# Scaled K and scaled R turned by one transposing DMA in place of two, and w_in loaded in three parts

## The chip, the cores and the metric

The kernel runs on one core of a Trainium2 chip. The core has five engines that run on their own and wait for each other through semaphores: PE (TensorE, matrix multiply), DVE (VectorE), ACT (ScalarE), POOL (GpSimd) and SP (SyncE, which only issues DMAs here). Sixteen DMA engines move data; SP's DMAs, POOL's DMAs and the fetches of the program itself all go through them. The metric is device time in microseconds, median of the runs shown; less is better.

## The reference

Two stages follow each other. The first is a linear attention with a decaying state, for 4 sequences of 768 steps, 8 heads of 48:

```
state = 0
for t in range(768):
    cur    = u * k[t] (outer) v[t]
    y[t]   = r[t] @ (state + cur)
    state  = w * state + k[t] (outer) v[t]
```

The second is a two-layer network on the 3072 rows of y (384 columns): `h = x @ w_in` (384 to 2048), a gate that is 0 below -1, h above 1 and (h+1)^2/4 between, and `g @ w_out` (2048 to 384). Inputs and output are float32.

## The kernel before

**Tiling.** The attention is done in chunks of 128 steps. There are 6 chunks and two pairs of sequences, so 12 groups g = 0 to 11; group g is chunk g // 2 of sequence pair g % 2. A group has two units (one sequence each), n = 2g and 2g + 1. Tokens of a unit stand on the 128 partitions when loaded: K, R and V of a group are 128 x 16 heads x 48 float32, three DMAs from SP (`load.K`, `load.R`, `loadV`; from group 2 on, one DMA for both units).

**Attention of a unit.** K and R are multiplied by tables of powers of w (L327), which gives Ks and Rs in bfloat16, padded from 48 to 64 columns a head so that two heads fill 128. Ks and Rs are turned (tokens from partitions to columns): for groups 0 to 2 on PE (L388, then a copy TT), from group 3 on by a transposing DMA from SP, one for Ks and one for Rs (step KRT, L398), each 128 x 1024 bfloat16. Then A = turned K times turned R (L406), its masked copy AT, Y = AT times V plus turned R times the state (L441, L446), and the state's update (Sp L432, Tm, decay). The bonus of u goes over KU, RKU, diag and V2 on POOL, DVE and ACT. y (L468) is Y + V2; from group 3 on both units' y stand in one tile yy and are turned by a further transposing DMA (xT, L511).

**Network of a group.** Per group: four quarters q of 512 hidden columns. mm1 (L526, 12 matmuls of 256 columns a quarter), relu and square on ACT, gate on DVE, then mm2 (L554) for each unit and quarter; `o` copies the result and `out` stores it. w_in lies whole in SBUF, loaded by POOL DMAs in W_IN = 2 parts of 1024 columns; w_out in 4 parts.

**Order.** The order of all work is written out by hand in the table ORDER: each token is one step, the digits behind its colon are buffer numbers, and each engine takes its own instructions in the order of the tokens. An engine, SP among them, stops at the first instruction whose wait is not fulfilled; what stands behind it on that engine stays back. Writing `KRT.K.4` means the turning DMA of Ks of group 4.

In the text a DMA is named by its step and group: KT.4 and RT.4 are the two turning DMAs of group 4, VF.3 is the load of V of group 3, xT.4 the turning of yy of group 4, w_out.2 the third part of w_out.

Of the kernel before, what the change touches and what calls it, by code (L numbers as in the profile page):

```python
# [36 lines left out]
lw loadV.0.0:0 bcw:1 load.K.1.1 KU.0.1@D loadV.0.1 wcol:0 Wdn_p:0 Ks.0.0@D:0 Wup_p load.R.1.1 Rs.0.0@D:0 wCm  # L37
KU.1.0@P:1 loadV.1.0:1 Ks.1.0@D:1 warm.4.h.2 T.0:1 load.K.2.0:2 Wdn RKU.1.0@P:1 Rs.1.0@D:1 Rs.0.1@D V.0.0@A:0
RKU.0.1@P T.2:2~3 TT.0@A:0 usum.0.0@D:0 Ks.1.1@D Ks.0.1@D KU.1.1@P Wup Sp.0:0 TT.2@D:1 A.0:1 V.0.1@A load.R.2.0:2
AT.0.1:0 RKU.1.1@P Tm.0@D Sp.1:1~5 T.1:2 Tm.1@D w_in.0 V.1.0@A:1 A.2:1 Rs.1.1@D loadV.1.1 Sp.2:0 AT.0.0 TT.1@D:2  # L40
usum.1.0@A:1 A.1:0~8 V2.0.0@P:0 Ks.2.0@P:2 AT.2.0:1 loadV.2.0:0 V2.1.0@A:1 Y.0:1 T.3:2 sbf.0@A Tm.2@D usum.0.1@D Y.2:0
TT.3@D:3 y.2:0 AT.1.1:2 Rs.2.0@P:2 A.3:1~14 X.2:0 V2.0.1@A y.0:1 AT.3.0:3 warm.2.h.2 X.0:1 T.5:2~8 AT.1.0 xT.2@A:0
T.4:0 TT.5@D:0 Y.1:0 w_in.1 load.K.3.0:0 xT.0@A:1 sbf.1@A usum.1.1@D A.5:1 mm1.0.0.0:2 KU.2.0@P:0 y.1:2 TT.4@D:1
load.R.3.0:0 V.1.1@A X.1:1 Y.3:0 AT.5.0:0 A.4:0 V2.1.1@P xT.1@A mm1.0.0.1 V.2.0@A:2 Sp.5:1 y.3:0 RKU.2.0@P:0
relu.0.0:0 X.3:0 Tm.5@D:0 mm1.0.1.0:1 AT.4.0:1 xT.3@A decay.5 square.0.0:0 usum.2.0@D:0 Sp.4:1 mm1.0.1.1 w_out.0 Y.4:0
relu.0.1:1 mm1.1.1.-1:0 gate.0.0:0 square.0.1:1 Tm.4@D:1 mm1.0.2.-1:2 relu.1.1:0 Y.5:1 square.1.1:0 V2.2.0@P:0 w_out.1
y.4:1 gate.0.1:1 w_out.2 X.4:0 w_out.3 mm1.0.3.-1:1 xT.4@A:2 gate.1.1:2 relu.0.2:1 Sp.3:0 y.5:2 mm1.1.0.-1:0
square.0.2:1 Tm.3@D KU.3.0@P:1 decay.4 gate.0.2:3 relu.0.3:0 relu.1.0:1 mm2.0.0.0:1 mm2.0.1.0:0 Ks.3.0@P:0
square.1.0:0 KRT.K.3:0 mm1.1.3.-1:2 mm2.0.1.1 Rs.3.0@P:0 RKU.3.0@P:1 mm2.0.0.1 square.0.3:1 gate.1.0:4 mm2.0.1.2 gate.0.3:5
relu.1.3:1 loadV.3.0:1 mm2.0.0.2 mm1.1.2.-1:0 square.1.3:0 usum.3.0@D:1 mm2.0.0.3 relu.1.2:0 KRT.R.3:0 mm2.0.1.3  # L50
o.0.0@D:0 square.1.2:1 mm2.1.0.0:1 o.0.1@D gate.1.3:6 load.K.4.0:1 X.5:0 mm2.1.0.1 load.R.4.0:1 xT.5@A V.3.0@A:3
mm1.2.3.-1:1 gate.1.2:7 sbf.3@A V2.3.0@P:1 Sp.7:0 A.7:2 loadV.4.0:0 relu.2.3:1 Tm.7@D:0 A.6:0 mm2.1.0.2 AT.6.0:2
sbf.2@A square.2.3:0 Ks.4.0@P:2 sbf.4@A Sp.6:0 mm2.1.0.3 load.K.5.0:2 Tm.6@D:1 mm1.2.0.-1:0 o.1.0@A:1 AT.7.0:3 decay.6
Y.6:0 Y.7:1 relu.2.0:0 KRT.K.4:1 y.6:0 mm1.2.1.-1:2 KU.4.0@P:0 y.7 V.4.0@A:4 gate.2.3:8 xT.6:1 RKU.4.0@P:0
square.2.0:1 mm2.1.1.0:0 Sp.8:1 mm2.1.1.1 load.R.5.0:2 Tm.8@D:1 relu.2.1:1 load.K.6.0:0 mm1.2.2.-1:1 gate.2.0:9
Ks.5.0@P:1 mm2.1.1.2 square.2.1:0 mm2.2.0.0:1 mm2.1.1.3 decay.7 Rs.4.0@P:1 mm1.3.0.-1:0 gate.2.1:0 relu.2.2:0
square.2.2:1 KRT.K.5:0 mm2.2.0.1 o.1.1@D sbf.5@A relu.3.0:1 mm1.3.1.-1:2 gate.2.2:1 out.1 KU.5.0@P:1 square.3.0:0
Rs.5.0@P:2 mm2.2.0.2 relu.3.1:0 gate.3.0:3 mm1.3.2.-1:1 KRT.R.4:1 square.3.1:1 loadV.5.0:1 load.R.6.0:0 usum.4.0@D:0
mm2.2.0.3 mm2.2.1.0:0 KU.6.0@P:0 relu.3.2:1 gate.3.1:5 mm1.3.3.-1:0 square.3.2:0 loadV.6.0:0 gate.3.2:4 mm2.2.1.1
V2.4.0@P:0 sbf.6@A o.2.0@A:1 A.9:2 sbf.7@A relu.3.3:0 A.8:1 AT.9.0:1 mm2.2.1.2 KRT.R.5:0 square.3.3:1 mm2.3.0.0:1  # L60
AT.8.0:0 out.0 decay.8 mm2.2.1.3 load.K.7.0:1 mm2.3.0.1 o.2.1@A gate.3.3:2 V.6.0@A:0 V.5.0@A:2 Y.8:0 Ks.6.0@P:0
mm2.3.0.2 y.8:1 Y.9:0 mm2.3.0.3 y.9 RKU.5.0@P:1 A.11:2 xT.8:0 o.3.0@A:0 A.10:1 usum.5.0@D:1 AT.11.0:2 mm2.3.1.0:0
Sp.10:1 KRT.K.6:1 mm2.3.1.1 Rs.6.0@P:0 RKU.6.0@P:0 Tm.10@D:0 mm2.3.1.2 load.R.7.0:1 Sp.9:1 mm2.3.1.3 Tm.9@D:1
V2.5.0@P:1 mm1.4.0.-1:0 AT.10.0:3 o.3.1@A sbf.8@A decay.9 decay.10 KRT.R.6:1 usum.6.0@D:0 relu.4.0:1 Sp.11:1 Y.10:0
mm1.4.1.-1:2 square.4.0:0 Tm.11@D:1 y.10:0 V2.6.0@P:0 Ks.7.0@P:2 Y.11:1 mm1.4.2.-1:1 loadV.7.0:0 out.2 relu.4.1:0
# [5 lines left out]
relu.5.1:1 xT.12:1 gate.5.2:8 mm2.4.1.0:1 KU.8.0@P:0 Sp.14:0 square.5.1:0 mm2.4.1.1 load.K.9.0:0 Tm.14@D:1 mm2.4.1.2
relu.5.3:0 sbf.10@A gate.5.1:3 mm2.5.0.0:0 Rs.8.0@P:2 A.15:2 square.5.3:1 A.14:0 AT.15.0:3 mm2.4.1.3 mm2.5.0.1
V.8.0@A:3 KRT.R.8:1 decay.13 RKU.8.0@P:0 AT.14.0:2 mm1.6.0.-1:2 o.4.1@A load.R.9.0:0 gate.5.3:5 Y.14:1 mm2.5.0.2
Ks.9.0@P:0 y.14:0 relu.6.0:1 mm1.6.1.-1:0 square.6.0:0 usum.8.0@D:0 gate.6.0:4 loadV.9.0:0 load.K.10.0:1 mm2.5.0.3
mm2.5.1.0:1 sbf.11@A sbf.12@A A.17:1 relu.6.1:0 o.5.0@D:0 KU.9.0@P:1 A.16:2 mm2.5.1.1 AT.17.0:0 V2.8.0@P:0 decay.14
Rs.9.0@P:0 square.6.1:1 sbf.13@A Y.15:0 mm2.5.1.2 mm1.6.2.-1:1 y.15 V.9.0@A:4 AT.16.0:1 xT.14:0 KRT.K.9:0 Sp.15:0
RKU.9.0@P:1 gate.6.1:2 mm2.5.1.3 load.R.10.0:1 mm1.6.3.-1:2 relu.6.2:1 square.6.2:0 relu.6.3:0 o.5.1@D Tm.15@D:0
mm2.6.0.0:1 gate.6.2:7 out.5 Y.16:0 mm1.7.1.-1:0 decay.15 square.6.3:1 y.16:1 KRT.R.9:0 Ks.10.0@P:2 Sp.17:0 Tm.17@D:1
gate.6.3:6 load.K.11.0:2 mm2.6.0.1 relu.7.1:1 mm1.7.0.-1:1 KU.10.0@P:0 square.7.1:0 sbf.15@A mm2.6.0.2 Sp.16:0
relu.7.0:0 KRT.K.10:1 loadV.10.0:1 gate.7.1:9 mm1.7.2.-1:2 Rs.10.0@P:1 Tm.16@D:0 mm2.6.0.3 square.7.0:1 o.6.0@A:0  # L80
sbf.14@A usum.9.0@D:1 Y.17:0 mm1.7.3.-1:0 decay.16 y.17 relu.7.2:1 gate.7.0:0 RKU.10.0@P:0 mm2.6.1.0:1 square.7.2:0
Sp.18:0 KRT.R.10:1 mm2.6.1.1 Tm.18@D:0 sbf.16@A decay.17 A.18:1 gate.7.2:1 out.4 mm2.7.0.0:0 relu.7.3:0 xT.16:2
KU.11.0@P:1 mm2.6.1.2 square.7.3:1 AT.18.0:2 V2.9.0@P:1 mm2.7.0.1 load.R.11.0:2 loadV.11.0:0 Ks.11.0@P:1 mm2.6.1.3
gate.7.3:3 mm2.7.0.2 A.21:2 sbf.17@A V.10.0@A:2 o.6.1@A A.19:1 AT.21.0:3 A.20:0 mm2.7.0.3 AT.19.0:1 out.6 Y.18:1
# [19 lines left out]
def kernel(  # L104
# [70 lines left out]
    for i in range(3):  # L175
        for x in padded:
            nc.vector.memset(padded[x][i][:, :, D:], 0.0)
# [472 lines left out]
```

## Time and profile before

| | us |
|---|---|
| median of 3 runs | 175.38 |
| lowest, highest | 174.95, 176.0 |
| span of the profiled execution | 176.4 |
| PE busy in it | 165.0 (94%) |
| DVE / ACT / POOL busy | 130.3 / 135.2 / 120.2 |
| clock granted to PE, mean over the span | 0.987 |
| SP's DMA queue (q1), POOL's (q0), share of 16 engines' span | 73.6% / 11.4% |

The profiled execution is given by its span alone; it is 1.0 us above the median and 0.4 us above the highest of the runs. Busy time of PE is modelled, so small waits can hide in it. DMA shares go by the time that packets were under way, two of which can overlap on an engine, so shares above 100% occur. A "group" line of the profile gives a line of the kernel, the engine, what is written and read, the count, busy time and the idle time just before.

### The profile page before, as it was taken

To read this page: it belongs to the slowest core of one execution; us is meant where nothing else is said; L and a number is where in the kernel's file an instruction comes from. 1 tells how busy PE (TensorE), PEld (TensorE's weight loads), DVE (VectorE), ACT (ScalarE), POOL (GpSimd) and SP (SyncE) were. 2 spreads that over 40 slices of the span, in tenths; PEclk is the share of its full clock that TensorE was granted. 3 is DMA by queue.
4 is the path that set the end of the run, shared out by engine and by line. 5 is a ranking of instruction groups with operands and counts; after the bars stand their busy time and mean duration, and the time that the engine had idled before them with its cause. 6 is when DMAs were issued, how large, how long until landed. Compare 5 with 4: busy or idle time off the path is not lost.

```text
span 176.4 us, 4159 instructions
## 1 busy us (share of the span) xinstructions
PE 165.0 (94%) x1684; PEld 125.2 (71%) x1684; DVE 130.3 (74%) x167; ACT 135.2 (77%) x194; POOL 120.2 (68%) x97
## 2 busy tenths in 40 slices
PE   6998699999999999779999999999999999999992
...
PEclk9999999999999999969999999999999999999998
DMA  5999999999999999996999997989982400312022
GB/s 109 221 219 192 216 175 234 207 165 209 238 172 196 191 202 252 158 183 175 196 221 211 185 183 159 266 149 243 194 197 93 89 17 4 97 37 89 4 89 89
DMA packets 106967, 28.78 MB, mean 163 GB/s; under 512 B 100930, under 2 KB 106180, under 8 KB 106948
## 3 DMA queue, kind: packets, MB, share of 16 engines
q1 hardware_dynamic: 103888, 25.24, 73.6%
q0 software_dynamic: 2912, 3.15, 11.4%
q8 instruction: 13, 0.21, 0.5%
...
q14 instruction: 6, 0.05, 0.1%
...
## 4 chain that ended last, share of the span: by engine, by line
PE 71%; DMA 13%; DVE 7%; ACT 5%; POOL 1%; issue 1%; DVEq 0%; POOLq 0%
PE hp L526 31%; PE op L554 30%; DMA VF<-in_v_dram 5%; DMA w_out_sb<-in_moe_w_out_dram 4%; DMA xT<-yy 3%; DVE AT L421 3%; PE A L406 2%; PE Y L446 2%; PE Y L441 2%; PE Sp L432 1%; ACT V L212 1%; PE ub L242 1%; POOL V L369 1%; PE wb L237 1%; ACT RKU L355 1%; DVE yy L468 1%
## 5 line engine op out<-in xcount | busy, mean ns | idle before, releaser
L526 PE MATMUL hp<-xT,w_in_sb 128*128 128x256 bf16 (+1 forms) x600 | 72.0, 271 | 3.4 <-DMA xT<-yy 2.2
L554 PE MATMUL op<-w_out_sb,gt 128*128 128x384 bf16 (+2 forms) x400 | 71.9, 320 | 0.1
L544 DVE SCALAR_TENSOR_TENSOR gt<-sq,hp 128x1024 bf16<-128x1024 f32 x48 | 57.9, 1216 | 16.2 <-ACT sq L539 16.1
L526 PEld LDWEIGHTS <-w_in_sb 128*128 128x128 bf16 x600 | 56.2, 99 | 13.9 <-issue 3.1
L534 ACT ACTIVATE pt<-hp 128x1024 f32<-128x1024 f32 x48 | 48.7, 1018 | 17.7 <-PE hp L526 17.4
L539 ACT ACTIVATE sq<-pt 128x1024 f32<-128x1024 f32 x48 | 50.4, 1057 | 1.2
L554 PEld LDWEIGHTS <-gt 128*128 128x128 bf16 x400 | 36.5, 98 | 19.3 <-issue 0.5
L421 DVE TENSOR_TENSOR AT<-A,umask 128x1024 bf16<-128x1024 f32 x22 | 26.5, 1218 | 2.2 <-PE A L406 1.9
L337 POOL TENSOR_TENSOR KU<-K,u_bc 128x768 f32<-128x768 f32 (+1 forms) x13 | 21.6, 1658 | 2.0 <-DVE u_bc L212 2.0
L344 POOL TENSOR_TENSOR RKU<-R,KU 128x768 f32<-128x768 f32 (+1 forms) x14 | 22.2, 1589 | 0.3
L489 POOL TENSOR_TENSOR state<-Tm,wCm 128x384 f32<-128x384 f32 x16 | 16.0, 1003 | 8.8 <-DVE Tm L476 8.6
L369 POOL TENSOR_TENSOR V<-V,diag 128x768 f32<-128x768 bf16 (+1 forms) x12 | 16.4, 1365 | 7.1 <-ACT V L212 4.7
L327 POOL TENSOR_TENSOR Ks<-Wdn,K 128x768 bf16<-128x768 f32 x10 | 18.2, 1818 | 1.2 <-DMA K<-in_k_dram 1.2
L327 POOL TENSOR_TENSOR Rs<-Wup,R 128x768 bf16<-128x768 f32 x10 | 18.2, 1819 | 0.1
L476 DVE TENSOR_TENSOR Tm<-Sp,state 128x384 f32<-128x384 f32 x16 | 8.9, 555 | 7.3 <-POOL Ks L327 3.4
L468 DVE TENSOR_TENSOR yy<-Y,V 128x384 bf16<-128x384 f32 x18 | 9.9, 554 | 5.0 <-PE Y L446 3.5
L212 ACT CAST V<-VF 128x768 bf16<-128x768 f32 (+1 forms) x14 | 10.2, 737 | 3.6 <-DMA VF<-in_v_dram 3.5
L446 PE MATMUL Y<-V,AT 128*128 128x48 bf16 x192 | 11.4, 185 | 1.2 <-POOL AT L416 0.9
L446 PEld LDWEIGHTS <-AT 128*128 128x128 bf16 x192 | 9.8, 98 | 2.8 <-POOL AT L416 1.3
L357 DVE TENSOR_REDUCE diag<-RKU 128x16 f32<-128x768 f32 (+1 forms) x13 | 11.1, 852 | 0.9 <-POOL RKU L344 0.9
L212 ACT COPY oo<-op 128x384 f32<-128x384 f32 x13 | 6.2, 476 | 6.7 <-PE op L554 6.3
L212 ACT CAST state_bf<-state 128x384 bf16<-128x384 f32 x20 | 10.0, 503 | 0.0
...
## 6 DMA issues: line engine op xcount, KB each, us to landing
...
```

The lines of the kernel that those rows point to most:

```text
L212: nc.scalar.copy(out, in_) if e == "A" else engines[e].tensor_copy(out, in_)
L327: engines[e].tensor_mul(of_unit(dst, j0, j1)[:, :, :, :D], rep(tab, j1 - j0), of_unit(tiles[what, g], j0, j1))
L337: engines[e].tensor_mul(of_unit(tiles["KU", g], j0, j1), of_unit(tiles["K", g], j0, j1), rep(u_bc, j1 - j0))
L344: engines[e].tensor_mul(of_unit(tiles["RKU", g], j0, j1), of_unit(tiles["R", g], j0, j1), of_unit(tiles["KU", g], j0, j1))
L369: engines[e].tensor_mul(tiles["V2", g][:, hs, :], tiles["V", g][:, hs, :], tiles["diag", g][:, hs].unsqueeze(2).to_broadcast([P, hs.stop - ...
L421: nc.vector.tensor_mul(t.rearrange("p i n t -> p (i n) t"), tiles.pop(("A", n)).rearrange("p i n t -> p (i n) t"), umask.unsqueeze(1).to_b ...
L446: nc.tensor.matmul(t[:, 2 * p + i, :], tiles["AT", n][:, i, p, :], tiles["V", g][:, j * H + 2 * p + i, :], start=(c == 0), stop=True, skip ...
L526: nc.tensor.matmul(hp[:, f, cols], w_in_sb[:, i, n0 : n0 + P], tiles["xT", g][:, units, i, :], start=(i == 0), stop=(i == nK - 1), skip_gr ...
L534: nc.scalar.activation(tiles["pt", g, q], tiles["hp", g, q], AF.Relu, bias=0.5, scale=0.5)
L539: nc.scalar.activation(tiles["sq", g, q], tiles.pop(("pt", g, q)), AF.Square, bias=0.0)
L544: nc.vector.scalar_tensor_tensor(out=gt, in0=tiles.pop(("sq", g, q)), scalar=1.0, in1=tiles.pop(("hp", g, q)), op0=ALU.min, op1=ALU.max)
L554: nc.tensor.matmul(t, tiles["gt", g, q][:, f, j * P : (j + 1) * P], w_out_sb[:, n, cols], start=(n == 0), stop=(n == nF - 1),)
```

## The change

There are four edits. (1) The padded buffers of Ks and Rs become one tile KRs (128 x 2 x 16 x 64) with Ks in its first half and Rs in its second; the six memsets of the padding on DVE become three of twice the width. (2) The step KRT turns the whole tile with one DMA (128 x 2048) into KRT, from which A and Y read K's and R's part. (3) In ORDER the token `KRT.K.g` is gone and `KRT.g` stands where `KRT.R.g` stood, which is behind the scaling of R. (4) W_IN lists column bounds: parts of 512, 512 and 1024 columns; `w_in.1` stands right behind `w_in.0`, and `w_in.2` where the second part stood.

```diff
-W_IN = 2
+W_IN = (0, 512, 1024, 2048)
 ...
-AT.0.1:0 RKU.1.1@P Tm.0@D Sp.1:1~5 T.1:2 Tm.1@D w_in.0 V.1.0@A:1 ...
+Tm.0@D Sp.1:1~5 T.1:2 Tm.1@D w_in.0 w_in.1 V.1.0@A:1 ...
 ...
-    padded = {x: [const.tile([P, UNITS * H, HP], BF16, name=x, tag=f"{x}{i}") for i in range(3)] for x in ("Ks", "Rs")}
+    padded = [const.tile([P, 2, UNITS * H, HP], BF16, name="KRs", tag=f"KRs{i}") for i in range(3)]
     for i in range(3):
-        for x in padded:
-            nc.vector.memset(padded[x][i][:, :, D:], 0.0)
+        nc.vector.memset(padded[i].rearrange("p k h d -> p (k h) d")[:, :, D:], 0.0)
 ...
     def w_in_go(e, bk, i):
-        n = slice(i * DF // W_IN, (i + 1) * DF // W_IN)
+        n = slice(W_IN[i], W_IN[i + 1])
 ...
     def scaled(e, bk, g, j, what):
         j0, j1 = span(g, j)
-        if j == 0:
-            tiles[what + "s", g] = padded[what + "s"][bk[0]]
+        if ("Ks", g) not in tiles:
+            tiles["KRs", g] = padded[bk[0]]
+            tiles["Ks", g], tiles["Rs", g] = padded[bk[0]][:, 0], padded[bk[0]][:, 1]
 ...
-        return tiles[what + "T", g][:, j * NP + p, :]
+        return tiles["KRT", g][:, "KR".index(what) * UNITS * NP + j * NP + p, :]
 ...
     @step
-    def KRT(e, bk, what, g):
-        t = tiles[what + "T", g] = buf(bk[0], [P, UNITS * NP, P], BF16, what + "T")
-        nc.sync.dma_start_transpose(out=t, in_=flat(tiles[what + "s", g]))
+    def KRT(e, bk, g):
+        t = tiles["KRT", g] = buf(bk[0], [P, 2 * UNITS * NP, P], BF16, "KRT")
+        nc.sync.dma_start_transpose(out=t, in_=tiles["KRs", g].rearrange("p k h d -> p (k h d)"))
```

The order of instructions moves on SP at nine places. The first is group 3. On SP before (names with buffer numbers; R_501 is the load of R of group 3, VF_779 that of V, KT_741 and RT_808 the two turnings, K_826 the load of K of group 4):

```order
L304 DMA K_467<-in_k_dram 128x16x48
L304 DMA R_501<-in_r_dram 128x16x48
L398 DMA_TRANSPOSE KT_741<-Ks_99 128x8x128
L304 DMA VF_779<-in_v_dram 128x16x48
L398 DMA_TRANSPOSE RT_808<-Rs_102 128x8x128
L304 DMA K_826<-in_k_dram 128x16x48
```

and the same place now (R_496 and VF_772 are the loads of R and V of group 3, KRT_801 the turning of both, K_819 the load of K of group 4):

```order
L301 DMA K_462<-in_k_dram 128x16x48
L301 DMA R_496<-in_r_dram 128x16x48
L301 DMA VF_772<-in_v_dram 128x16x48
L396 DMA_TRANSPOSE KRT_801<-KRs_99 128x16x128
L301 DMA K_819<-in_k_dram 128x16x48
```

The load of V of group 3 stood behind KT.3, which waits for POOL's scaling of K; now it stands right behind the load of R, and the turning follows it.

The second place is the turning of groups 4 and 5 and the turning of yy of group 4 on SP. Before (KT_1062 and RT_1194 are group 5, RT_1114 is group 4, xT_1273 is xT.4, K_1211 and R_1315 loads of group 7, KT_1300 is group 6):

```order
L398 DMA_TRANSPOSE KT_1062<-Ks_100 128x8x128
L587 DMA out_0_dram<-oo_925 128x2x384
L398 DMA_TRANSPOSE RT_1114<-Rs_103 128x8x128
L304 DMA VF_1118<-in_v_dram 128x16x48
L304 DMA R_1120<-in_r_dram 128x16x48
L304 DMA VF_1154<-in_v_dram 128x16x48
L398 DMA_TRANSPOSE RT_1194<-Rs_104 128x8x128
L587 DMA out_0_dram<-oo_814 128x2x384
L304 DMA K_1211<-in_k_dram 128x16x48
L511 DMA_TRANSPOSE xT_1273<-yy_1242 128x6x128
L398 DMA_TRANSPOSE KT_1300<-Ks_99 128x8x128
L304 DMA R_1315<-in_r_dram 128x16x48
```

and now (KRT_1103, KRT_1183 and KRT_1336 are groups 4, 5 and 6, xT_1262 is xT.4, K_1200 and R_1302 the loads of group 7):

```order
L585 DMA out_0_dram<-oo_918 128x2x384
L396 DMA_TRANSPOSE KRT_1103<-KRs_100 128x16x128
L301 DMA VF_1107<-in_v_dram 128x16x48
L301 DMA R_1109<-in_r_dram 128x16x48
L301 DMA VF_1143<-in_v_dram 128x16x48
L396 DMA_TRANSPOSE KRT_1183<-KRs_101 128x16x128
L585 DMA out_0_dram<-oo_807 128x2x384
L301 DMA K_1200<-in_k_dram 128x16x48
L509 DMA_TRANSPOSE xT_1262<-yy_1231 128x6x128
L301 DMA R_1302<-in_r_dram 128x16x48
L396 DMA_TRANSPOSE KRT_1336<-KRs_99 128x16x128
```

The K halves have moved back to the places of the R halves, and behind xT.4 stands a load where a turning stood.

The third place is POOL at the first part of w_in. Before:

```order
L344 TENSOR_TENSOR RKU_209<-R_156,KU_187 128x384
L290 DMA w_in_sb_66<-in_moe_w_in_dram 128x3x1024
L416 AFFINE_SELECT AT_255<-AT_255 128x1024
L369 TENSOR_TENSOR V2_327<-V_213,diag_230 128x384
L327 TENSOR_TENSOR Ks_101<-Wdn_127,K_206 128x16x48
```

and now:

```order
L342 TENSOR_TENSOR RKU_203<-R_150,KU_181 128x384
L287 DMA w_in_sb_66<-in_moe_w_in_dram 128x3x512 x2
L414 AFFINE_SELECT AT_249<-AT_249 128x1024
L367 TENSOR_TENSOR V2_322<-V_207,diag_224 128x384
L325 TENSOR_TENSOR KRs_101<-Wdn_121,K_200 128x16x48
```

Two DMAs of half the columns stand on POOL where one stood; the rest of POOL's order is as it was.

More of the change, by code (lines that the diff above doesn't have):

```diff
@@ L36 @@
 warm.18 load.K.0.0:0 load.R.0.0:0 load.K.0.1 load.R.0.1 load.K.1.0:1 load.R.1.0:1 bcu:0 u_bc@D KU.0.0@P:0 RKU.0.0@P:0
[L37 to L65, printed above, removed]
@@ L71 @@
[L71 to L84, printed above, removed]
-o.7.0@A:1 y.18:0 mm1.8.0.-1:2 relu.8.0:1 KRT.K.11:0 AT.20.0:0 Y.19:0 mm1.8.1.-1:1 y.19 mm2.7.1.0:1 square.8.0:0
```

78 lines of the change are left out of this document (60 added, 18 removed).

## The prediction

> **What bounds the kernel now.** I read the page's first two parts, then the chain of waits, then the stretches in which PE is not busy.
>
> ```profile
> span 176.4 us, 4159 instructions
> PE 165.0 (94%) x1684; PEld 125.2 (71%) x1684; DVE 130.3 (74%) x167; ACT 135.2 (77%) x194; POOL 120.2 (68%) x97
> ...
> PE   6998699999999999779999999999999999999992
> ...
> PEclk9999999999999999969999999999999999999998
> DMA  5999999999999999996999997989982400312022
> ```
>
> A slice is 4.4 us. PE is full from slice 5 (22 us) on, with one hole at slices 16 and 17 (70 to 79 us), where its clock drops too. The DMA engines are full from the start to about 110 us. So there are three stages: a start up to 40 us that hangs on DMA, a middle up to 80 us in which PE is full but for one hole, and the rest, which is PE alone. A change to DMAs can matter in the start and at the hole. The chain, cut to 14 to 42 us, shows what the start hangs on:
>
> ```profile
> 28.04 1.47 POOL V L369
> 29.50 0.76 POOL w_out_sb L294
> 30.26 7.92 DMA w_out_sb<-in_moe_w_out_dram
> 38.22 1.46 PE op L554 x8
> ```
>
> The start ends when w_out.2 has landed at 38.18 and PE's second layer reads it. The 7.92 us are mostly queueing: the DMA queues in 27 to 30 us and in 30.5 to 37.5 us (packets, MB, share) were
>
> ```profile
> q1 hardware_dynamic: 3500, 0.67, 113.0%
> q0 software_dynamic: 42, 0.05, 10.0%
> ```
>
> ```profile
> q0 software_dynamic: 1836, 1.37, 127.9%
> ```
>
> First SP's queue (q1: K and R of group 3) has the engines to itself, although w_out.0 was issued at 26.91 (below); then POOL's (q0: w_out) has them, 262 packets a us, so 1.95 us for each of its four parts of 512 packets.
>
> The hole, by the chain, PE's timeline, and stretches (length, busy time of PE, PEld, DVE, ACT, POOL, then clock, DMA share, GB/s):
>
> ```profile
> 69.89 6.13 DMA xT<-yy
> ```
>
> ```profile
> 73.07 0.81 PE L554 MATMUL op<-w_out_sb,gt 128*128 128x384 bf16 x4
> 76.06 2.72 PE L526 MATMUL hp<-xT,w_in_sb 128*128 128x256 bf16 x12 [2.18 <-DMA xT<-yy]
> ```
>
> ```profile
> 74.00:75.00 1.00, 0.00 (x0) 0.00 (x0) 1.00 (x2) 0.81 (x2) 1.00 (x2) 1.00 0.00 0
> ```
>
> ```profile
> 75.00:80.00 5.00, 3.94 (x33) 3.15 (x33) 1.61 (x3) 1.15 (x2) 4.96 (x4) 0.66 0.91 177
> ```
>
> PE waits 2.18 us for xT.4, and then gets 0.66 of its clock over 5 us, which loses 0.34 x 5 = 1.7 us more: 3.9 us in all. xT.4 took 6.13 us where its kind takes 2.7 to 2.8 (below), and in 74 to 75 us no DMA packet started at all. What stopped them? The DMA view of 73.2 to 73.3 us and of 60.5 to 61.5 us, the other place where packets of a turning DMA stopped:
>
> ```profile
> q8 instruction: 1, 0.02, 108.6%
> ```
>
> ```profile
> q8 instruction: 1, 0.02, 5.9%
> ```
>
> ```profile
> q8 instruction: 13, 0.21, 0.5%
> ```
>
> Both times one packet of the instruction queue (the last row is the page's: 13 packets, 16 KB each, about one for each 259 of PE's 1684 matmuls and as many weight loads) went out while a turning DMA was under way, and the turning stood still until it was through. I read it so: a turning goes in step over all engines, so one engine held by a fetch holds all. The fetch comes when PE reaches a certain instruction; xT.4 comes when yy is done. Whether they meet is a matter of some tenths of a us, and this decides 3.9 us.
>
> **The change part by part.** The turning DMAs, by tile:
>
> ```profile
> L398 SPq DMA_TRANSPOSE KT<-Ks x9: 1242/1324/3627, 36.3 to 127.6; - x9
> ...
> DMA to landing us min/median/max: 2.8/4.5/5.4
> ```
>
> ```profile
> DMA to landing us min/median/max: 2.7/4.7/5.5
> ```
>
> ```profile
> DMA to landing us min/median/max: 2.7/2.8/6.1
> ```
>
> The fences are KT, RT and xT. An issue of 256 KB keeps SP for 1.24 us at least. I take twice that for the whole tile (2.5 us; the same rows would have to be described), so nine turnings fewer save SP nothing, and the DMA engines move the same packets. Bounds: nothing is saved, or 9 x 1.24 = 11 us of SP, which waits much of its time anyway. On the path either counts zero, except at the following places.
>
> *Start: V of group 3 goes ahead of w_out.* SP's timeline:
>
> ```profile
> 22.46 4.37 SPq L304 DMA_DIRECT2D R<-in_r_dram  x1
> 36.34 1.32 SPq L398 DMA_TRANSPOSE KT<-Ks  x1
> 37.78 0.51 SPq L304 DMA_DIRECT2D VF<-in_v_dram  x1
> ```
>
> SP stood from 26.83 to 36.34 in front of KT.3, which waits for POOL, with VF.3 behind it. Without KT.3, VF.3 is issued at 26.83, eleven us earlier. It is 2048 packets, which at 3500 in 3 us are 1.75 us of all engines, and now they fall between the loads of group 3 and w_out, whose landing PE waits for. If SP's queue goes first, as it did in 27 to 30 us, w_out moves by 1.75 us; if the two take turns, packet for packet, by what passes while w_out.0 to .2 go, three quarters of it, 1.3 us. Lower end 0 (the engines would have to have room; the share of 127.9% speaks against it), upper end 1.75. I take 1.6, nearer the first, since that is what the 42 packets of q0 show. What is gained: V of group 3 is cast earlier, which lets POOL's V2.3 start earlier, in front of Ks.4, which waits for K of group 4 anyway: zero.
>
> *Start: one more DMA on POOL.* POOL's timeline:
>
> ```profile
> 13.26 0.93 POOL L290 DMA_DIRECT2D w_in_sb<-in_moe_w_in_dram  x1
> ...
> 26.91 0.80 POOL L294 DMA_DIRECT2D w_out_sb<-in_moe_w_out_dram  x1
> 28.04 1.47 POOL L369 TENSOR_TENSOR V<-V,diag 128x768 f32<-128x768 bf16 x1 [0.32 <-DVE diag L357]
> ```
>
> 0.8 to 0.9 us more, less the 0.32 idle, leave 0.5 at w_out's issue. That issue already waited for the DMA engines (42 packets by 30 us), so it is hidden while SP's queue is full; I take 0.2 of 0 to 0.9. *w_in in halves:* PE waited 0.5 us for the first part, so 0 to -0.5. *Memsets:*
>
> ```profile
> PE hp L526 <- DMA w_in_sb<-in_moe_w_in_dram: 0.8, 2, 0.5
> ```
>
> ```profile
> L177 DVE MEMSET Ks<- 128x128 uint32 x3 | 0.5, 165 | 0.0
> ```
>
> six of 0.165 become three of up to double: 0 to -0.5, ahead of a stage that waits for DMA. I take -0.2 for both. The start becomes 1.6 + 0.2 - 0.2 = 1.6 us longer, range -1.0 to 2.65 by the ends, of which I use 0.4 to 2.7, since the full queues are in the rows.
>
> *Middle: the K halves come later.* KRT.5 stands in RT.5's place, with K's 256 KB added; before, KT.5 had gone ahead of the loads between.
>
> ```profile
> 64.96 2.58 SPq L398 DMA_TRANSPOSE RT<-Rs  x1
> ...
> 68.21 0.46 SPq L304 DMA_DIRECT2D K<-in_k_dram  x1
> 69.89 2.08 SPq L511 DMA_TRANSPOSE xT<-yy  x1
> ```
>
> ```profile
> 69.85 0.62 PE L406 MATMUL A<-RT,KT 48*128 48x128 bf16 x16
> ```
>
> RT.5 landed about 64.96 + 4.7 = 69.7, and A of group 5 starts at 69.85: it has no slack. The other half adds at most 1.24 us (the time in which so much is issued), so 70.9. But with the start longer by 1.6, PE comes to A at 71.45. So it costs nothing, covered by 0.5 us; without the cover, up to 1.1.
>
> *Middle: the hole.* All that follows PE moves by 1.6: yy and the issue of xT.4 to 71.5, the fetch to 74.8, PE's need from 73.88 to 75.5. What follows SP and the loads does not move: K.7 in front of xT.4 is issued at 68.21 to 69.5. So xT.4 finds its queue shorter and lands at 71.5 + 2.8 = 74.3, before the fetch, and behind it stands the load of R where KT.6 stood. The hole closes: -3.9 us. Bounds: 0 (they meet again) and -3.9.
>
> How large the second part of the hole is can be weighed. The stretch from 75 to 80 us has the clock at 0.66 after an idle of 2.18 us. The Trainium skill ("TensorE: Matmul & The Clock Gate", Part 1: The HAM clock gate) says that PE falls to half its clock after an idle window of about 3.4 us, by which a wait of 2.18 us would mostly leave the clock alone. This trace disagrees, since the clock fell; by that rule the hole would be worth 2.2 us, and the sum would end at 174.8.
>
> *Rest.* After 80 us the page's row has PE at 9 tenths or more in every slice, and the DMA engines fall from full to 4 tenths and less. A turning that is later by up to 1.24 us is taken as covered by the matmuls of the network that stand between; if one is not, PE waits up to that long, once.
>
> **Sum.** 176.4 + 1.6 + 0 - 3.9 = 174.1 us of span, 2.3 less than the profiled execution. The runs' median is 1.0 below that span, so 175.38 - 2.3 = 173.1.
>
> **Rivals.** *(A) The hole stays.* Its place is xT.4 against the fetch at 74.8. My margin is 0.5 us; if the start grows by less than about 1.0 us, or KRT.5 pushes K.7 and with it xT.4 by more than 0.5, they meet as before and PE pays both: 175.38 + 1.6 = 177.0. For it: the tenths. The same time comes if the timed runs had no hole at all, for which the span above every run speaks, though only by 0.4 where 3.9 would be due. *(B) The start costs nothing and the hole closes:* w_out takes no harm (start -0.2), and KRT.5, now uncovered, costs 0.5 of its 0 to 1.1, which also moves the fetch back: 175.38 - 3.9 + 0.3 = 171.8. The full queues speak against it. The Trainium skill ("DMA: Bandwidth & Descriptors", Rules for kernel authors) advises to coalesce small transfers into a large one, which would make each pair of turnings cheaper for the engines; it would lead to this case. No row here shows a price by size: the 192 KB of xT and the 256 KB of KT both land in 2.7 to 2.8 us at best, which agrees with a fixed part but leaves open whether a full queue hides it. *(C) Gain and loss cancel,* the start longer by 2.7 and the hole closed to a third, or the hole half as wide: about 175.4.
>
> **How the numbers follow.** Forecast 0.42, at 173.1, its own range 171.9 to 174.4 (start 0.4 to 2.7, and 0.2 about it). A 0.30 (176.3 to 177.8), B 0.12, C 0.16. The range leaves out the last parts of B and A: 171.4 to 177.4. By about 0.5%, 0.88 us, a run of this kernel can be told from no change: faster is the forecast and B, 0.53; within 0.5% is C and a little of A, 0.17; slower the rest of A, 0.30.
>
> **What would show it.** VF.3 issued near 27 us, with SP's queue (q1) at over 1500 packets between 30 and 37 us and w_out.2 landing near 40: the start is right; w_out.2 at 38.2 or sooner says B. KRT near 2.5 us of issue on SP. No idle of PE before A of group 5. xT.4 landing within 3.5 us, no PE idle before its first layer and a clock of 1.0 from 75 to 80: the hole is closed; a wait for xT of over 1.5 us says A. The prediction is wrong in its reasons if PE shows a new idle stretch after 85 us, or if the start's length stays and the time falls all the same.

## The result: slower by 0.7%

The changed kernel takes 175.93 us in the median of 20 runs (175.14 to 176.4), the kernel before beside it 174.64 us (173.68 to 176.0, 20 runs). The ratio is 1.0072, with a 95% interval of 1.0054 to 1.0091: slower by 1.3 us. The prediction was 173.1, faster.

The page of the kernel after, its span, PE's busy row, PE's clock and the DMA row in 40 slices:

```profile
span 174.0 us, 4130 instructions
PE 164.6 (95%) x1684; PEld 125.9 (72%) x1684; DVE 130.7 (75%) x164; ACT 135.4 (78%) x194; POOL 120.6 (69%) x98
...
PE   7996989998999999999999999999999999999991
...
PEclk9998799999999999999999999999999999999999
DMA  5999999999996999999999998999922700402022
```

The span is 174.0, where the sum of the prediction gave 174.1. There is no hole at slices 16 and 17. The clock dips once, at slices 3 and 4 (13 to 22 us), which the page of the kernel before did not show. This execution took 175.67 us, that is 1.7 more than its span, and the same 1.7 stands between span and time in all 20 runs of it. By the same distance the profiled execution of the kernel before, with a span of 176.4, took some 178.1 us (an estimate, as its time is not on record). That is 3.5 above the median of that kernel: it was an outlier, and the hole is what made it one (before_twice, below).

**The start.** PE's timeline of the kernel after, around its use of w_out.2, and SP's from the same stretch:

```profile
37.25 1.46 PE L552 MATMUL op<-w_out_sb,gt 128*128 128x384 bf16 x8
39.86 1.46 PE L552 MATMUL op<-w_out_sb,gt 128*128 128x384 bf16 x8 [1.14 <-DMA w_out_sb<-in_moe_w_out_dram]
```

```profile
27.00 3.69 SPq L301 DMA_DIRECT2D VF<-in_v_dram  x1
38.49 4.43 SPq L396 DMA_TRANSPOSE KRT<-KRs  x1
```

VF.3 is issued at 27.00 (37.78 before), and PE waits 1.14 us for w_out.2 and uses it at 39.86 (38.22 before). The DMA queues of the kernel after in 30.5 to 37.5 us, then the landing of VF.3 (the last number is us from issue to landing):

```profile
q0 software_dynamic: 1407, 1.06, 96.8%
q1 hardware_dynamic: 1528, 0.29, 32.3%
```

```profile
VF<-in_v_dram SPq DMA_DIRECT2D x1, 384.0 KB, 16.1
```

In the profile shown of before, w_out had these seven us nearly alone, with 1836 packets. Now 1407 of it pass beside 1528 of SP's queue. These counts alone do not prove a delay: in before_twice, a second profile of the kernel before, 1443 of w_out pass beside 2021 in the same seven us, and PE does not wait. There SP's packets come early, between 31 and 33 us, and w_out has the engines behind them. What tells the two apart is the stretch from 34 to 39 us, in the kernel after and then in before_twice:

```profile
q0 software_dynamic: 976, 0.73, 92.6%
q1 hardware_dynamic: 970, 0.19, 33.6%
```

```profile
q0 software_dynamic: 1225, 0.91, 118.9%
q1 hardware_dynamic: 357, 0.09, 18.9%
```

In the kernel after the two queues pass packet for packet, and w_out gets 195 packets a us in place of 245. VF.3 gains nothing: issued 11 us sooner it lands at 27.00 + 16.1 = 43.1, as it did before (43.1, with 5.3 us under way).

**The middle.** The turnings of the kernel after (KRT, all nine: issue time min/median/max in ns; who waited; landing), then PE at the place of the hole, and the clock in 75 to 80 us:

```profile
L396 SPq DMA_TRANSPOSE KRT<-KRs x9: 1317/2392/4490, 38.5 to 134.8; - x9
...
who waited for it (us, times):
  PEld L404: 0.3, 1
...
DMA to landing us min/median/max: 3.7/5.3/6.6
```

```profile
74.46 0.81 PE L552 MATMUL op<-w_out_sb,gt 128*128 128x384 bf16 x4
75.11 1.47 PE L524 MATMUL hp<-xT,w_in_sb 128*128 128x256 bf16 x12
```

```profile
75.00:80.00 5.00, 5.00 (x66) 4.38 (x64) 4.37 (x7) 4.21 (x6) 4.82 (x5) 1.00 1.22 176
```

No matmul waits for a turning, and none for xT.4; a weight load waits 0.3 us once, for KRT.6. The clock is full here.

### The profile page after: what moved, and what is told of

The parts are those of the page before. It is cut to its first block, busy times and chain, and to the rows that moved or that the text cites. A ratio compares the mean times of both kernels' runs of the same rounds, so it can differ in the third digit from the quotient of the medians.

```text
span 174.0 us, 4130 instructions
## 1 busy us (share of the span) xinstructions
PE 164.6 (95%) x1684; PEld 125.9 (72%) x1684; DVE 130.7 (75%) x164; ACT 135.4 (78%) x194; POOL 120.6 (69%) x98
## 4 chain that ended last, share of the span: by engine, by line
PE 72%; POOL 9%; DMA 7%; SPq 4%; DVE 3%; issue 2%; DVEq 0%; POOLq 0%
PE op L552 33%; PE hp L524 31%; DMA w_out_sb<-in_moe_w_out_dram 5%; SPq L301 4%; PE A L404 3%; DMA R<-in_r_dram 2%; DVE AT L419 2%; POOL KRs L325 2%; PE Y L444 2%; PE Y L439 2%; POOL V L367 2%; POOL RKU L342 2%; POOL w_in_sb L287 1%; PE Sp L430 1%; POOL AT L414 1%
## 5 line engine op out<-in xcount | busy, mean ns | idle before, releaser
L524 PE MATMUL hp<-xT,w_in_sb 128*128 128x256 bf16 (+1 forms) x600 | 70.8, 268 | 1.0 <-DVE AT L419 0.4
L524 PEld LDWEIGHTS <-w_in_sb 128*128 128x128 bf16 x600 | 55.6, 98 | 10.8 <-issue 0.8
L487 POOL TENSOR_TENSOR state<-Tm,wCm 128x384 f32<-128x384 f32 x16 | 16.1, 1007 | 6.1 <-DVE Tm L474 6.0
L325 POOL TENSOR_TENSOR KRs<-Wdn,K 128x768 bf16<-128x768 f32 x10 | 18.2, 1821 | 0.0
L325 POOL TENSOR_TENSOR KRs<-Wup,R 128x768 bf16<-128x768 f32 x10 | 18.2, 1820 | 0.0
L209 ACT CAST V<-VF 128x768 bf16<-128x768 f32 (+1 forms) x14 | 10.2, 738 | 1.9 <-DMA VF<-in_v_dram 1.9
```

What stands on the lines that cost most here:

```text
L209: nc.scalar.copy(out, in_) if e == "A" else engines[e].tensor_copy(out, in_)
L325: engines[e].tensor_mul(of_unit(dst, j0, j1)[:, :, :, :D], rep(tab, j1 - j0), of_unit(tiles[what, g], j0, j1))
L524: nc.tensor.matmul(hp[:, f, cols], w_in_sb[:, i, n0 : n0 + P], tiles["xT", g][:, units, i, :], start=(i == 0), stop=(i == nK - 1), skip_gr ...
```

## The experiments

Theories. **S**: the early VF.3 takes DMA engines from w_out, which PE waits for; this is the loss. **P**: the third DMA of w_in on POOL delays all that POOL does behind it. **M**: the merged turning itself is late. And on the other side of the sum, **H1**: the hole was in the profiled execution of before alone; **H2**: it is in the timed runs too, and the change closed it.

All ratios are to the kernel before, run beside on the same chip, with 95% intervals. "us" is the median. The kernel before itself had medians from 174.07 to 174.66 us on the chips used, so rows are compared by their ratios.

| run | what differs | us | ratio |
|---|---|---|---|
| kernel after | the change | 175.93 | 1.0072 (1.0054 to 1.0091) |
| before_twice | kernel before, again | 174.62 | 1.0013 (0.9991 to 1.0034) |
| vf3_early | before, VF.3 early | 175.81 | 1.0070 (1.0044 to 1.0096) |
| before_w_in_three | before, w_in in three | 174.42 | 1.0025 (1.0002 to 1.0049) |
| w_in_two | after, w_in in two | 175.51 | 1.0050 (1.0032 to 1.0067) |
| vf3_back | after, VF.3 behind KRT.3 | 175.43 | 1.0056 (1.0034 to 1.0077) |
| merge_alone | after, VF.3 behind KRT.3, w_in in two | 174.77 | 1.0048 (1.0029 to 1.0067) |
| merge_r7_behind | the same, R of group 7 behind KRT.6 | 174.37 | 1.0024 (1.0007 to 1.0042) |
| merge_v3_pool | after, VF.3 on POOL's queue, w_in in two | 174.33 | 0.9983 (0.9958 to 1.0009) |
| after_v3_pool | after, VF.3 on POOL's queue | 175.08 | 1.0035 (1.0008 to 1.0061) |
| before_v4_first | before, VF.4 ahead of R of group 4 | 174.50 | 0.9980 (0.9950 to 1.0009) |
| merge_v3_pool_v4 | merge_v3_pool with VF.4 and R of group 7 moved | 174.04 | 0.9973 (0.9953 to 0.9993) |
| fetch_moved | before, 14 more idle matmuls at 17 us | 174.23 | 1.0006 (0.9986 to 1.0026) |

A second table serves as a ruler. The gate on DVE writes the tile gt 48 times, always in the same order; these are the starts (us) of the 8th (PE has just passed the start), the 12th, the 16th (ahead of xT.4), the 17th (behind it) and the last, in the profiled executions:

| | 8th | 12th | 16th | 17th | 48th |
|---|---|---|---|---|---|
| before, first profile | 43.93 | 56.21 | 66.83 | 80.97 | 169.82 |
| before_twice | 43.71 | 56.78 | 67.22 | 77.62 | 166.35 |
| after | 45.68 | 57.96 | 68.58 | 78.76 | 167.30 |
| vf3_early | 45.04 | 57.32 | 67.94 | 78.27 | 167.62 |
| w_in_two | 45.91 | 58.19 | 68.81 | 79.00 | 167.48 |
| before_w_in_three | 43.71 | 56.91 | 67.34 | 77.53 | 165.99 |
| vf3_back | 44.46 | 57.04 | 67.67 | 78.66 | 168.23 |
| merge_alone | 43.78 | 57.17 | 67.60 | 77.78 | 166.26 |
| merge_v3_pool | 43.96 | 56.43 | 67.05 | 77.23 | 165.87 |
| after_v3_pool | 44.33 | 56.79 | 67.41 | 77.61 | 166.09 |
| fetch_moved | 43.09 | 55.36 | 65.98 | 77.33 | 165.80 |

### Is the hole in every execution? (before_twice)

> The kernel before, unchanged, to see whether its profiled execution has the hole at xT.4 (PE idle 2.18 us, clock 0.66) each time. Theory H1 (the hole is a meeting of some tenths of a us, which the profile of before had and the timed runs mostly have not): no wait of PE for xT.4 here, a span of 172.5 to 173.5, and the ratio 1.000. Theory H2 (the hole is in all executions, timed ones too, and the change closed it, so that something else cost 4 us more): a wait for xT.4 of about 2 us and a span of 176 again.

Measured: 174.62 us, ratio 1.0013. The page of this second profile of the same kernel, and the stretch from 75 to 80 us:

```profile
span 172.9 us, 4159 instructions
...
PE   6999789999989999998999999999999999999991
...
PEclk9999999999999999999999999999999999999999
```

```profile
75.00:80.00 5.00, 4.91 (x69) 4.07 (x67) 4.18 (x7) 4.52 (x6) 4.97 (x5) 1.00 0.95 178
```

H1 holds. There is no wait for xT.4 and no lost clock, and the span is 172.9, with a time of 174.65. In the ruler the step from the 16th to the 17th gate is 10.40 us here, 14.14 in the first profile: the hole cost 3.7 us there, and it is not the usual case. Of the 120 runs of the kernel before that stood beside the kernels of this study, three are above 177 us (177.63, 177.65 and 178.98), where a run with such a hole would lie; what held these three up is not on record.

### The early load alone (vf3_early)

```diff
-Ks.3.0@P:0 square.1.0:0 KRT.K.3:0 mm1.1.3.-1:2 ... relu.1.3:1 loadV.3.0:1 mm2.0.0.2
+Ks.3.0@P:0 square.1.0:0 loadV.3.0:1 KRT.K.3:0 mm1.1.3.-1:2 ... relu.1.3:1 mm2.0.0.2
```

> The kernel before, with nothing changed but the load of VF.3 put ahead of KT.3 on SP. Theory S: w_out.2 lands at 39.5 to 39.9 in place of 38.2, PE reads it there, the start is 1.3 to 1.6 us longer and so is the time: 175.9 to 176.2, ratio 1.007 to 1.009. Rivals P and M: POOL's and the turnings' DMAs are as before, so 174.6, ratio 1.000.

Measured: 175.81 us, ratio 1.0070. SP's and PE's timelines:

```profile
27.25 2.66 SPq L304 DMA_DIRECT2D VF<-in_v_dram  x1
35.68 5.45 SPq L398 DMA_TRANSPOSE KT<-Ks  x1
```

```profile
36.83 1.46 PE L554 MATMUL op<-w_out_sb,gt 128*128 128x384 bf16 x8 [0.47 <-DMA w_out_sb<-in_moe_w_out_dram]
39.26 1.46 PE L554 MATMUL op<-w_out_sb,gt 128*128 128x384 bf16 x8 [0.97 <-DMA w_out_sb<-in_moe_w_out_dram]
```

One token moved, and nothing merged, makes a loss as large as that of the whole change: 0.47 + 0.97 us of waiting for w_out, and the 8th gate at 45.04, 1.33 later than in before_twice. S holds as a sufficient cause. The size is not all from the start: of the 1.33 us 0.8 is given back by the 12th gate (below), and in this profile 0.6 is lost again behind the 17th (89.35 us from there to the last gate, 88.73 in before_twice). That part is not explained.

### Putting the load back (vf3_back, merge_alone)

In vf3_back the token goes behind the turning of group 3; merge_alone has w_in in two parts besides.

```diff
-relu.1.3:1 loadV.3.0:1 mm2.0.0.2 ... relu.1.2:0 KRT.3:1 mm2.0.1.3
+relu.1.3:1 mm2.0.0.2 ... relu.1.2:0 KRT.3:1 loadV.3.0:1 mm2.0.1.3
```

> The changed kernel, with the load of VF.3 put back behind the turning DMA of group 3 (KRT.3). Theory S (the early VF.3 takes DMA engines from w_out, and that is the whole loss): VF.3 is issued behind 42 us, SP's queue is empty while w_out goes, w_out.2 lands at 38.2 to 38.9 in place of 39.8, PE reads it there, and the time is that of the kernel before, 174.6 +- 0.5 (ratio 0.997 to 1.003). Rival P (the third DMA of w_in holds POOL back, and with it the issue of w_out): the time stays at 175.9, ratio 1.007. Rival M (the merged turning itself costs it, in group 3 or later): also 175.9, but with PE's use of w_out.2 back at 38.2 to 38.9. What may blur it: VF.3 now comes some 5 us later than in the kernel before (behind a longer turning), so V2.3 on POOL may be late.

> The changed kernel with w_in in two parts as before, and with VF.3 back behind KRT.3: of the change only the merged turnings are left, without the early load. w_out goes as in the kernel before, and the start is its start: PE uses w_out.2 at 38.2. Theory T (one turning of 512 KB lands later than the second of two of 256 KB, and this shows once the start is as short as before): KRT.6 lands at 80.5 to 81, A of group 6 waits for it 0.6 to 1.2 us, and the time is 175.0 to 175.6, ratio 1.003 to 1.007. Rival (the wait of 1.03 us for KRT.6 that the run with VF.3 held back showed was a chance of its profiled execution, in which an instruction fetch fell into that turning): no wait there, and the time is 174.2 to 174.7, ratio 0.999 to 1.002.

Measured: 1.0056 and 1.0048. S in its simple form fails: the start is short again (8th gate at 44.46 and 43.78, against 45.68), but most of the loss stays. The two profiles show different things. In vf3_back PE waited for KRT.6:

```profile
81.04 0.40 PE L404 MATMUL A<-KRT 48*128 48x128 bf16 x8 [1.03 <-DMA KRT<-KRs]
```

That wait belongs to this execution, which took 176.6 us, the longest of its ten; in merge_alone KRT.6 landed at 79.01 and A of group 6 starts at 79.07, so that there is no such wait, but no slack either. A fetch of instructions lies inside KRT.6 in both (76.43 and 75.42), so it is not what tells them apart. What both have in common is group 3. ACT in merge_alone, then in before_twice, at the cast of V.3:

```profile
44.36 0.83 ACT L209 CAST V<-VF 128x768 bf16<-128x768 f32 x1 [0.73 <-DMA VF<-in_v_dram]
```

```profile
43.46 0.83 ACT L212 CAST V<-VF 128x768 bf16<-128x768 f32 x1
```

Behind KRT.3, VF.3 is 0.9 late for its cast. The distance from the 8th gate to the first mask of group 3 on DVE is 2.45 and 2.39 us in these two, 2.14 in before_twice. In merge_alone there is one more wait, near 52 us:

```profile
52.23 0.33 PE L430 MATMUL Sp<-V,KRs 128*128 128x96 bf16 x4 [0.51 <-ACT V L209]
```

This is the cast of V.4, which waits for VF.4; before_twice has such a wait too (0.44, shown below). From the 8th to the 12th gate merge_alone needs 13.39 us and before_twice 13.07. So 0.3 us of the loss has a place, most of it behind VF.3; the rest of the 0.7 is not located by these profiles. The finding gives a sharper theory, V: with one turning in place of two, SP's queue has no good place left for VF.3. Ahead of KRT.3 it falls on w_out; behind it, it is late for V.3.

### Giving the load a place of its own (merge_v3_pool)

```diff
-        nc.sync.dma_start(out=tiles[what, g][:, j0 * H : j1 * H, :], in_=src)
+        (nc.gpsimd if (what, g) == ("VF", 3) else nc.sync).dma_start(out=tiles[what, g][:, j0 * H : j1 * H, :], in_=src)
 ...
-W_IN = (0, 512, 1024, 2048)
+W_IN = (0, 1024, 2048)
 ...
-w_out.2 X.4:0 w_out.3 mm1.0.3.-1:1
+w_out.2 X.4:0 w_out.3 loadV.3.0:1 mm1.0.3.-1:1
 ...
-gate.0.3:5 relu.1.3:1 loadV.3.0:1 mm2.0.0.2
+gate.0.3:5 relu.1.3:1 mm2.0.0.2
```

The tokens of w_in go back to two parts with it (w_in.0 and, further on, w_in.1).

> The changed kernel with w_in in two parts, and with the load of VF.3 on POOL's queue right behind w_out.3: there it can't take engines from w_out, and it need not wait for KRT.3. Theory V (what the merged turnings cost is a place for VF.3: on SP it goes either ahead of w_out or behind KRT.3, where it lands at 44.3 and the cast of V.3 is 0.9 late): w_out.2 is used near 38.2, VF.3 lands by 43, the cast of V.3 starts by 43.5, A of group 3 comes 2.1 us behind the last gate ahead of it as in the kernel before, and the ratio is 0.998 to 1.003. Rival M (the merged turnings cost 0.5% at other places): ratio 1.004 to 1.007. POOL has 0.75 us more to do in front of the scaling of group 3, so KRT.3 is issued near 38.8; if that shows, A of group 3 waits for it up to 0.7.

Measured: 0.9983 (0.9958 to 1.0009). POOL, PE (w_out.1 and .2 in one row) and the cast of V.3:

```profile
31.68 1.20 POOL L301 DMA_DIRECT2D VF<-in_v_dram  x1
```

```profile
36.68 2.76 PE L552 MATMUL op<-w_out_sb,gt 128*128 128x384 bf16 x16
39.28 1.47 PE L524 MATMUL hp<-xT,w_in_sb 128*128 128x256 bf16 x12
```

```profile
43.90 0.83 ACT L209 CAST V<-VF 128x768 bf16<-128x768 f32 x1
```

VF.3 goes behind w_out.3 in one and the same queue, w_out has no wait, the cast of V.3 does not wait for its data, and the 0.5 to 0.7% is gone with the merged turnings in place; the interval does not meet that of merge_alone. V holds as to the time, with two limits. The mask of group 3 stands 2.33 us behind the 8th gate, not the 2.1 expected, as PE now waits 0.46 us for DVE at 42.5. And SP's queue has one load fewer, so that VF.4 too is issued sooner (43.47, 44.00 in before_twice) and the wait at 52 us is gone: from the 8th to the 12th gate it is 12.47 us. The fair partner is therefore the kernel before with VF.4 moved (below), at 0.9980. Beside it the merged turnings cost nothing that these runs can tell. M as the cause of the 0.5% falls, as KRT.6 is as tight here as in merge_alone (it lands at 78.63, A starts at 78.68); by the widths of the intervals a cost of some 0.3% would not show.

### w_in in three parts (before_w_in_three, w_in_two, after_v3_pool)

```diff
-W_IN = 2
+W_IN = (0, 512, 1024, 2048)
 ...
-Tm.1@D w_in.0 V.1.0@A:1
+Tm.1@D w_in.0 w_in.1 V.1.0@A:1
```

This is before_w_in_three, in which the old w_in.1 becomes w_in.2 at its place; w_in_two undoes it in the kernel after; after_v3_pool is the kernel after with VF.3 moved to POOL as above and w_in left in three parts.

> The kernel before with w_in in parts of 512, 512 and 1024 columns and nothing else. POOL issues one DMA more, so the mask of A (AT) and all behind it on POOL come 0.7 later, w_out.0 is issued at 27.5 and not 26.8. Theory S: PE waits 1.3 us for the mask near 16 us in place of 0.2 to 0.7, the clock falls there, and w_out.2 is used near 38.7; the time rises by 0.2 to 0.6, to 174.7 to 175.1. Rival P (this is the cause of the loss): 175.7 to 175.9. Rival (hidden as in the changed kernel): 174.5, ratio 1.000.

> The changed kernel with w_in in two parts as before, so that the merged turnings alone are left of the change. Theory S: VF.3 is still early, so w_out.2 lands near 39.5, and the time is 175.6 to 175.9 (ratio 1.005 to 1.007). Rival P: w_out is issued 0.7 earlier, at 26.9, and the time falls back to 174.6 to 175.0 (ratio 1.000 to 1.002).

> The changed kernel whole (merged turnings and w_in in three parts), with one thing moved: the load of VF.3 on POOL's queue right behind w_out.3. Theory V (the place of VF.3 is the cause of the loss): w_out.2 is used at 38.2 to 38.9 and the ratio to the kernel before is at most 1.002, against 1.007 of the changed kernel. What w_in in three parts adds shows beside the ratio 0.998 of the same kernel with two parts: 0.000 to 0.003 more. Rival (w_in in three parts and the merge hurt together what neither does alone): 1.004 to 1.007.

Measured: 1.0025 in the kernel before; 1.0050 for the kernel after without it, beside 1.0072 with it; 1.0035 beside 0.9983 where VF.3 is on POOL's queue. Each pair gives 0.2 to 0.5%, and in none are the intervals far apart, so the sign is likely and the size is not known well. The wait can be seen in the profiles. PE in before_w_in_three and in the kernel after at the first product with a mask, and the stretch from 15 to 22 us in before_twice and after (the number behind POOL's is the clock):

```profile
15.79 0.37 PE L446 MATMUL Y<-V,AT 128*128 128x48 bf16 x8 [0.99 <-POOL AT L416]
```

```profile
16.16 0.50 PE L444 MATMUL Y<-V,AT 128*128 128x48 bf16 x8 [1.43 <-POOL AT L414]
```

```profile
15.00:22.00 7.00, 5.67 (x106) 4.59 (x103) 6.05 (x11) 6.31 (x24) 6.98 (x7) 1.00 1.13 208
```

```profile
15.00:22.00 7.00, 5.75 (x86) 5.33 (x86) 4.74 (x9) 6.46 (x25) 7.00 (x6) 0.76 1.20 205
```

The extra DMA stands on POOL right in front of the mask that PE waits for. In the kernels that have three parts and the merged turnings, PE waits 1.3 to 1.5 us there and then has 0.76 of its clock; with two parts it waits up to 0.7 with the clock at 1.00. That this wait makes the loss, the profiles do not show. In before_w_in_three it was 0.99 us, the clock stayed at 1.00 (a fall had been expected), and the 8th gate starts at 43.71, as in before_twice. In w_in_two, without the third part, the 8th gate is no sooner than in the kernel after (45.91, 45.68). In the 20 runs of the kernel after, the clock mostly did not fall, and runs in which it may have are no longer (last section), so the clock is not the cost. In after_v3_pool, where no wait for w_out stands behind it, the 8th gate is 0.37 later than in merge_v3_pool and the last 0.22, of some 0.9 us that the ratios differ by. after_v3_pool at 1.0035 also missed the 1.002 that V allowed it, so that a joint effect of the two edits is not excluded. P is likely as a second, smaller cause, and its place is open.

### The queue ahead of KRT.6 (merge_r7_behind)

```diff
-mm2.3.1.2 load.R.7.0:1 Sp.9:1 ... KRT.6:0 usum.6.0@D:0
+mm2.3.1.2 Sp.9:1 ... KRT.6:0 load.R.7.0:1 usum.6.0@D:0
```

> As the run with the merged turnings alone, and the load of R of group 7 stands behind KRT.6 on SP in place of ahead of it. Theory T: KRT.6 then has 2048 packets, some 1.75 us of the engines, fewer ahead of it and lands near 79; A of group 6 does not wait, and the time is that of the kernel before, 174.2 to 174.7. Rival (the queue ahead does not matter, KRT.6 is late since it waits for the scaling of R, or R of group 7 becomes late in its place, since POOL scales it at 82.2): 175.0 to 176, with a wait of PE for KRT.6 or KRT.7.

Measured: 1.0024, half the loss of merge_alone, intervals overlapping (1.0007 to 1.0042 and 1.0029 to 1.0067). No profile of either has a wait for KRT.6. In this one KRT.6 lands at 75.79, 2.8 us ahead of A of group 6, where merge_alone has no slack. Whether the timed runs of merge_alone had such waits stays open, and this run is inconclusive.

### Does a fetch of instructions make the hole? (fetch_moved)

```diff
-AT.3.0:3 warm.2.h.2 X.0:1
+AT.3.0:3 warm.16.h.2 X.0:1
```

> The kernel before with 14 more idle matmuls on PE near 17 us, where it waits anyway: the program has 28 more instructions on PE there, so that, if the fetch of instructions comes at a certain count of them, it comes some 1.2 us earlier against PE's work from there on (rates near 70 us: 24 instructions a us). It came 0.4 us after xT.4 had landed in the repeated run of the kernel before (74.26 against 73.86). Theory (a fetch that falls into a turning DMA stops it): the fetch falls near 73, into xT.4's flight, xT.4 takes 5 to 6 us, PE waits about 2 us and its clock falls, in most executions: 177 to 178.5, ratio 1.014 to 1.022. Rival (the hole of the first profile had another cause than the fetch, or the fetch is not tied to the count of instructions): 174.5 to 174.9 and no wait for xT.4.

Measured: 174.23 us, ratio 1.0006: no loss. The profile shows the two steps of the theory all the same. The queues in 71.5 to 71.8 us, PE's timeline, and the landing times of the nine turnings xT:

```profile
q8 instruction: 1, 0.02, 19.7%
```

```profile
73.67 1.47 PE L526 MATMUL hp<-xT,w_in_sb 128*128 128x256 bf16 x12 [0.99 <-DMA xT<-yy]
```

```profile
DMA to landing us min/median/max: 2.7/2.8/4.6
```

More instructions ahead brought the fetch forward, from 74.2 in before_twice to 71.6 (PE itself is 1.2 us ahead there), into the flight of xT.4 (issued at 69.05). xT.4 took 4.6 us and PE waited 0.99 us for it. In the eight profiles in which xT.4 was issued as quickly (1.2 us) and had no fetch inside, it took 2.8 to 3.1 us. While the fetch was under way no packet started at all for a stretch (72.25 to 72.50 us), as from 74 to 75 us in the first profile. From the 16th to the 17th gate this execution needs 11.35 us, the undisturbed ones 10.2 to 10.4: the hole cost 1.1 us, not 3.7, as the clock stayed at 1.00. In this execution it is made up for: PE came to the place 1.2 us earlier than in before_twice (16th gate at 65.98), 0.6 of it from the start and 0.8 from the stretch around 52 us, which it passed without a wait. Whether the timed runs had the wait is not on record. So the mechanism is supported by two profiles, and my size for it (2 to 3.5 us in most executions) was wrong.

### Another wait that the short start uncovers (before_v4_first, merge_v3_pool_v4)

With a short start, PE reaches group 4 before its V. PE in before_twice:

```profile
51.84 0.33 PE L432 MATMUL Sp<-V,Ks 128*128 128x96 bf16 x4 [0.44 <-ACT V L212]
```

From the 8th to the 12th gate before_twice needs 13.07 us, the kernel after 12.28, vf3_early 12.28. So 0.8 us of what the longer start costs is given back here.

```diff
-mm2.1.0.1 load.R.4.0:1 xT.5@A ... A.7:2 loadV.4.0:0 relu.2.3:1
+mm2.1.0.1 loadV.4.0:0 load.R.4.0:1 xT.5@A ... A.7:2 relu.2.3:1
```

> The kernel before, with the load of VF.4 ahead of that of R of group 4 on SP. In the repeated run of the kernel before, and in all runs with a short start, PE waits 0.3 to 0.6 us near 52 us for the cast of V.4, which waits 1.2 us for VF.4, and the distance from the 9th to the 12th gate is 6.5 to 6.8 us in place of 5.9. Theory: VF.4 lands 1.5 us sooner, the wait goes, and the time falls by 0.4 to 0.8: ratio 0.995 to 0.998. Rival (R of group 4 becomes late in its place, or another floor stands right behind): ratio 0.999 to 1.003.

> The run with VF.3 on POOL's queue, and with both of the other moves: VF.4 ahead of R of group 4, and R of group 7 behind KRT.6. If the moves add, it is the fastest of all, 0.4 to 0.8 below the kernel before (ratio 0.995 to 0.998); if the merged turnings cost something that no place of the loads mends, it is slower than the kernel before with VF.4 moved, by 0.3% or more.

Measured: 0.9980 (0.9950 to 1.0009), not told from no change, and 0.9973 (0.9953 to 0.9993) for the version with all moves. In before_v4_first the wait is gone:

```profile
50.96 0.81 PE L554 MATMUL op<-w_out_sb,gt 128*128 128x384 bf16 x4
51.61 0.33 PE L432 MATMUL Sp<-V,Ks 128*128 128x96 bf16 x4
```

The last version is the fastest of the study: merged turnings, w_in in two parts, VF.3 on POOL's queue, VF.4 and KRT.6 ahead of the loads of R. It beats the kernel before by 0.3% and, going by the two ratios, the kernel after by 1%. It is not told from merge_v3_pool.

## Why the prediction was wrong

*The start, longer by 1.6 us (0.4 to 2.7): right.* w_out.2 was used 1.64 later than in the profile shown, and PE's wait for it, the reason given, is 1.14 of that; PE came there 0.5 late. With the early load alone (vf3_early) it was used 1.04 later. So the load is nearer 1.1 than 1.6 and the rest of the start nearer 0.5 than 0; that the sum came out is luck in part. Of the two ways in which the queues could share, they took turns: 976 packets of w_out beside 970 of SP's queue in 34 to 39 us. The Trainium skill ("DMA: Bandwidth & Descriptors", Queues, rings and completion order) says that an engine takes turns between the queues it has work for, a packet each. These counts agree. The 42 packets of the prediction had made me lean to SP's queue going first; whether w_out had packets ready in 27 to 30 us, the trace does not show. In the timed runs 1.3 us arrived; up to 0.8 us came back where PE no longer waited for V.4; that wait was not in the profile I read, as PE was late there by other causes.

*POOL's extra DMA at 0.2, w_in in halves and the memsets at -0.2, nothing together: too low.* PE's wait at 16 us for the mask, which the DMA now stands in front of, was not in my list. The DMA and the halves together cost 0.2 to 0.5% by the runs, 0.2% of it in the kernel after, with overlapping intervals; which of the terms was off is not shown, and the memsets were not run alone.

*Middle, KRT.5 later but covered: right.* It landed at 70.65 (70.9 summed), A of group 5 starts at 71.60 (71.45 summed) and did not wait. The limit named, "without the cover, up to 1.1", was met once, at KRT.6 in vf3_back (1.03 us).

*The turning of the whole tile at 2.5 us of issue: near by luck.* The median is 2.39, but the 2.5 was twice the least time of half the size, 1.24, and the least of the whole tile is 1.32. The nine turnings keep SP for 25.6 us in all, the eighteen of before for 37.5, so that SP does save time, 12 us; the kernel's time shows nothing of it.

*The hole closes, -3.9 us: right of the two traces, wrong of the time.* xT.4 landed at 74.53 (74.3 summed), before the fetch at 76.44 (74.8 summed), and the span fell from 176.4 to 174.0 as summed (174.1). But before_twice has xT.4 ahead of the fetch too, without the change (73.87 and 74.26), so it is not shown that the change closed the hole. Its size was also read too simply: of xT.4's 6.13 us not all that is above 2.8 is the fetch's, as xT.4 took 3.4 to 4.2 us in the four profiles in which its issue too was held up (1.5 to 2.3 us) with no fetch inside.

**The step that failed is the last of the sum:** "The runs' median is 1.0 below that span, so 175.38 - 2.3 = 173.1". It carries a gain that the profiled execution alone could make over to runs that had nothing to gain: the -3.9 of the hole was worth about nothing to them. A span is shorter than the time of its own execution, by 1.7 us in every run whose span is on record here; a span that lies above the median of the times was the sign that this execution lost some 3 us that the others did not. I saw the sign and priced it at 0.4; the distance of 1.7 was not on record with the three runs that I had. With the hole taken out first, the same terms give the start alone: the case that I had placed in rival A, "if the timed runs had no hole at all", 177.0, or +1.6. Measured was +1.3. The base hid a part of the miss: 175.38 was the median of three runs, and the 20 runs of the same kernel have 174.64, so that the change in time was off by 3.6 us and the time itself by 2.8.

One reading was loose as well: the DMA row of the kernel before is full to about 132 us, with two dips, not to 110. No term hangs on it.
